# Sinkhorn attention, Fourier mixing and MLP on one core: every batch kept on chip, V made mean-free, the Fourier transform folded and taken along the sequence first, the MLP of one batch interleaved with the next

## Chip, cores and metric

One core of one Trainium2 chip. The metric is the device time of one execution in microseconds (us), the median of several runs; profiles are single executions. Engines are named as in the profile: PE is the matrix engine, PEld its weight load, DVE VectorE, ACT ScalarE, POOL GpSimd, SP SyncE. Line numbers such as L286 are lines of the kernel that was profiled, so an experiment with added lines has other numbers.

## The reference, cut to what matters

```python
B, H, S, D = 4, 8, 768, 64; n_blocks = 8; block = 96           # q, k, v are float32, 0.1 * randn
P = sort_net                                                    # [B, H, 8, 8]
for _ in range(5):                                              # Sinkhorn: softmax rows, then columns
    P = exp(P - max(P, -1)); P = P / sum(P, -1); P = P / sum(P, -2)
k_sorted = einsum('bhij,bhjcd->bhicd', P, k_blocks)             # mix the 8 blocks of a head
v_sorted = einsum('bhij,bhjcd->bhicd', P, v_blocks)
attn = softmax(q_block @ k_sorted_block.T / 8)                  # 96 x 96, block by block
x = (attn @ v_sorted_block) -> [B, S, 512]
mixed = real(fft(fft(x, axis=1), axis=2))                       # 768 x 512, per batch
u = x + mixed
un = (u - mean(u)) / sqrt(var(u) + 1e-6)
out = u + relu(un @ w_ch1) @ w_ch2                              # 512 -> 2048 -> 512
```

## The kernel before

It works in stages, each over all four batches. The mix matrices are built from the Sinkhorn result by 48 small copies between on-chip tiles. Mixed K and V go to DRAM and come back in another layout. The Fourier transform runs along the features first (tables of 257 columns, the rest mirrored), then along the sequence with all 768 rows as contraction. `u` goes to DRAM and is fetched again by the MLP, which is the last stage.

```python
    for t in range(2):                                  # mix matrices, by DMA
        for i in range(NB):
            e.dma_start(pc[:, i:i + 1], pw[16 * t:16 * t + 16, i:i + 1, :])
        nc.vector.memset(lpf, 0.0)
        for g in range(16):
            e.dma_start(lpf[8 * g:8 * g + 8, 8 * g:8 * g + 8], pc[8 * g:8 * g + 8, :])
    # ... q loaded and transposed ...
            for t in range(2):                          # K: rows are (b h i), columns (c d)
                nc.gpsimd.dma_start(cin, kv[128 * t:128 * (t + 1), :])
                for n in range(NTIL):
                    nc.tensor.matmul(ps, lhsPk[t], cin[:, 512 * n:512 * (n + 1)])
                    evict(n, oo[:, 512 * n:512 * (n + 1)], ps)
                nc.sync.dma_start(ks_dram[128 * t:128 * (t + 1), :], oo)
    # ... V the same in float32, with the sums over c for the mean path; back to vs_dram ...
            for b in range(B + 1):                      # attention, one batch behind its scores
                    nc.sync.dma_start(kssb[...], ks_dram[...])
                    nc.scalar.dma_start(vspb[...], vs_dram[...])
                # ... transposes, scores, exp - 1, eTm1 @ V, 1/sum, the mean put back ...
    # ... Fourier for each batch: 48 matmuls of 257 columns, then per 128 rows:
                for sc in range(6):
                    nc.tensor.matmul(pU, cs16_sb[:, sc, 128 * ic:128 * ic + 128],
                                     T1[b][:, sc, :], start=False, stop=False)
                    nc.tensor.matmul(pU, ssn16_sb[:, sc, 128 * ic:128 * ic + 128],
                                     T2[b][:, sc, :], start=False, stop=(sc == 5))
                nc.sync.dma_start(u_dram[6 * b + ic], u)
                # ... normalize, transpose into unT ...
    with tc.tile_pool(name="mlp", bufs=1) as mlp:       # the MLP of all batches, last
        for st in range(6):
            for fc in range(16):
                # 4 matmuls of 512 columns, relu on ACT
            for sc in range(4):
                # 16 matmuls of 512 columns
                nc.sync.dma_start(ur, u_dram[gidx])
                nc.vector.tensor_tensor(ot, pc2, ur, op=ALU.add)
```

The softmax here doesn't subtract the row's maximum and nothing guards it: scores larger than these inputs give would overflow.

## Time and profile before

539.37 us (median of 3 runs, 538.71 to 539.91).

| stage | stretch, us | PE busy, us | granted PE clock | what it is limited by |
|---|---|---|---|---|
| prologue: mix matrices, K and V mix, q transposes | 0 to 112 | 42.2 | 0.95 (no record before 60.1 us) | transfers, on the chain |
| attention | 112 to 232 | 91.6 | 0.50 | small matmuls at half clock |
| Fourier and normalization | 247 to 365 | 113.0 | 1.00 | PE |
| MLP | 365 to 536 | 165.8 | 1.00 | PE |

From the page of the kernel before, busy time by engine and slices of 1/40 of the span; a digit is the busy share in tenths, `PEclk` the granted clock:

```profile
PE 426.2 (80%) x2524; PEld 225.4 (42%) x2524; DVE 221.1 (41%) x750; ACT 184.7 (34%) x502; POOL 56.7 (11%) x85
...
PE   0500698127695959998999999998999999999996
...
PEclk9999999755555555559999999999999999999999
DMA  9999258799707073117951112122231313140502
```

PE is empty in places in the first fifth, at half clock in the second, and full after that. The table by stretch, kernel before:

```profile
core 0: us, PE busy (x) PEld busy (x) DVE busy (x) ACT busy (x) POOL busy (x), PEclk, DMA share, GB/s
0.00:112.00 112.00, 42.24 (x170) 19.44 (x170) 49.40 (x171) 26.24 (x79) 25.00 (x35) 0.95 1.06 195
112.00:232.00 120.00, 91.58 (x790) 60.52 (x792) 66.68 (x267) 57.30 (x155) 26.06 (x42) 0.50 0.52 62
247.00:365.30 118.30, 112.95 (x736) 65.43 (x736) 81.69 (x260) 42.83 (x169) 1.31 (x2) 1.00 0.37 100
365.30:535.70 170.40, 165.84 (x770) 74.97 (x767) 16.95 (x26) 57.47 (x98) 0.00 (x0) 1.00 0.25 75
```

What holds the prologue is read from the chain that ended last (start, length, what), kernel before:

```profile
1.26 14.71 DMA qsb_196<-in_q_dram
...
29.06 11.05 DMA pc_132<-pw
...
46.74 5.19 DMA lhsPf_141<-pc_132
...
103.79 7.90 DMA vspb_793<-vs_dram
112.10 6.32 DMA kssb_792<-ks_dram
```

These are a load of q, then the small copies that build the mix matrices and the way back from DRAM. The copies and the way back are the pieces that the change removes.

### The profile page before, as it was taken

Reading aid. Unit: us, or ns where it says so; the run is one execution under the profiler, and the core shown is the slowest. Engines: PE = TensorE matmul, PEld = TensorE weight load, DVE = VectorE, ACT = ScalarE, POOL = GpSimd, SP = SyncE. Lnnn points to the kernel's source line nnn. Section 1 sums busy time; section 2 is a strip of 40 time slices with the busy share of each in tenths; the row PEclk is TensorE's granted clock in tenths of the full one; section 3 lists DMA queues with packets and bytes.
Section 4 is the critical chain, followed back from the end, with each engine's and each line's share of the span. In section 5 each row is a group of like instructions: output and inputs, shape, how many; then the busy total and the mean of one; then the engine's idle time right before and its main releaser. Section 6 shows DMA issues by size and latency. Waiting matters only on the chain.

```text
span 535.7 us, 7003 instructions
## 1 busy us (share of the span) xinstructions
PE 426.2 (80%) x2524; PEld 225.4 (42%) x2524; DVE 221.1 (41%) x750; ACT 184.7 (34%) x502; POOL 56.7 (11%) x85
## 2 busy tenths in 40 slices
PE   0500698127695959998999999998999999999996
PEld 0300253014463645654646464643444444444442
DVE  1610589414474655865667676672111101010101
ACT  1400452019643719005514142325243333324240
POOL 5613000100041230541000000000000000000000
PEclk9999999755555555559999999999999999999999
DMA  9999258799707073117951112122231313140502
GB/s 319 196 198 112 89 185 319 169 118 147 48 2 59 1 56 115 49 50 221 202 138 51 69 61 77 42 80 98 46 113 40 118 39 119 21 137 6 152 0 80
DMA packets 95043, 55.46 MB, mean 104 GB/s; under 512 B 80664, under 2 KB 82720, under 8 KB 93472
## 3 DMA queue, kind: packets, MB, share of 16 engines
q1 hardware_dynamic: 35776, 29.53, 20.2%
q0 software_dynamic: 28416, 10.52, 16.6%
q10 hardware_dynamic: 30816, 14.96, 14.0%
q8 instruction: 20, 0.33, 0.3%
q14 instruction: 15, 0.12, 0.1%
HBM read 46.55 MB, written 18.94 MB: 122 GB/s over the span
## 4 chain that ended last, share of the span: by engine, by line
PE 67%; DMA 13%; DVE 9%; ACT 5%; issue 2%; ACTq 2%; SPq 1%; POOL 0%; DVEq 0%; POOLq 0%
DMA qsb_196<-in_q_dram 3%; DMA pc_132<-pw 2%; ACTq L288 2%; DMA vspb_793<-vs_dram 1%; DMA qsb_279<-in_q_dram 1%; DMA kssb_792<-ks_dram 1%; SPq L188 1%; DMA pc_159<-pw 1%; PE ps_2747 L386 1%; DMA lhsPf_141<-pc_132 1%; DMA vspb_2007<-vs_dram 1%; DMA vspb_1043<-vs_dram 1%; PE ps_5472 L499 1%; PE ps_5406 L499 1%; PE ps_5265 L499 1%
## 5 line engine op out<-in xcount | busy, mean ns | idle before, releaser
L491 PEld LDWEIGHTS <-w1sb 128*128 128x128 f16 x384 | 37.5, 98 | 45.1
L230 PE MATMUL ps_372<-pkin_369,lhsPk 128*128 128x512 f16 x1 | 0.6, 606 | 29.9 <-DVE lhsPk L220 29.9
L454 PEld LDWEIGHTS <-ssn_sb 128*128 128x128 f16 x144 | 14.1, 98 | 17.0
L452 PEld LDWEIGHTS <-cs_sb 128*128 128x128 f16 x144 | 14.0, 97 | 17.1
L230 PEld LDWEIGHTS <-lhsPk 128*128 128x128 f16 x12 | 1.5, 132 | 33.8 <-DVE lhsPk L220 30.2
L156 PE MATMUL ps_207<-ident,qsb_196 128*128 128x128 f16 x1 | 0.3, 289 | 16.0 <-DMA qsb_196<-in_q_dram 16.0
L156 PEld LDWEIGHTS <-kssb_792 128*128 128x128 f16 x24 | 2.5, 138 | 22.9 <-issue 22.9
L146 ACT CAST pkout_371<-ps_372 128x512 f16<-128x512 f32 x1 | 0.6, 585 | 32.9 <-DMA lhsPf_168<-pc_159 32.9
L220 DVE CAST lhsPk<-lhsPf_141 128x128 f16<-128x128 f32 x1 | 0.2, 227 | 27.0 <-DMA lhsPf_168<-pc_159 27.0
L156 PEld LDWEIGHTS <-qsb_196 128*128 128x128 f16 x24 | 2.1, 131 | 19.0 <-DMA qsb_196<-in_q_dram 19.0
L156 PE MATMUL ps_815<-ident,kssb_792 128*128 128x128 f16 x1 | 0.3, 266 | 12.2 <-DMA vspb_793<-vs_dram 12.2
L499 PEld LDWEIGHTS <-hr_5124 128*128 128x128 f16 x64 | 6.3, 98 | 7.5
L499 PEld LDWEIGHTS <-hr_4384 128*128 128x128 f16 x64 | 6.3, 98 | 7.5
L499 PEld LDWEIGHTS <-hr_4754 128*128 128x128 f16 x64 | 6.3, 98 | 7.5
L499 PEld LDWEIGHTS <-hr_4569 128*128 128x128 f16 x64 | 6.3, 98 | 7.5
L499 PEld LDWEIGHTS <-hr_4939 128*128 128x128 f16 x64 | 6.3, 98 | 7.5
L499 PEld LDWEIGHTS <-hr_5309 128*128 128x128 f16 x64 | 6.3, 98 | 7.5
L270 POOL DMA_DIRECT2D a_781<-a_dram x4 | 2.2, 567 | 55.5 <-DMA a_dram<-a_615 48.0
L505 DVE TENSOR_TENSOR ot_4500<-ps_4481,ur_4498 128x512 f32<-128x512 f32 x1 | 0.7, 692 | 17.0 <-PE ps_4481 L499 17.0
L505 DVE TENSOR_TENSOR ot_4685<-ps_4666,ur_4683 128x512 f32<-128x512 f32 x1 | 0.7, 692 | 16.6 <-PE ps_4666 L499 16.6
L505 DVE TENSOR_TENSOR ot_5055<-ps_5036,ur_5053 128x512 f32<-128x512 f32 x1 | 0.7, 692 | 16.6 <-PE ps_5036 L499 16.6
L505 DVE TENSOR_TENSOR ot_5425<-ps_5406,ur_5423 128x512 f32<-128x512 f32 x1 | 0.7, 692 | 16.6 <-PE ps_5406 L499 16.6
(2847 smaller groups left out, 1344.6 us busy)
## 6 DMA issues: line engine op xcount, KB each, us to landing
w1sb<-in_moe_w_ch_dram POOLq DMA_DIRECT2D x1, 2048.0 KB, 16.1
w2sb<-in_moe_w_ch_dram POOLq DMA_DIRECT2D x1, 2048.0 KB, 27.0
pvin_616<-in_v_dram SPq DMA_DIRECT2D x1, 1536.0 KB
pvin_656<-in_v_dram SPq DMA_DIRECT2D x1, 1536.0 KB
pkin_369<-in_k_dram POOLq DMA_DIRECT2D x1, 1536.0 KB, 12.6
pkin_409<-in_k_dram POOLq DMA_DIRECT2D x1, 1536.0 KB, 19.0
ks_dram<-pkout_371 SPq DMA_DIRECT2D x1, 1536.0 KB
ks_dram<-pkout_411 SPq DMA_DIRECT2D x1, 1536.0 KB
```

What stands on the lines that cost most here:

```text
L146: nc.scalar.copy(dst, src)
L156: nc.tensor.matmul(ps[:nn, :kk], src_ap, idt[:kk, :kk], is_transpose=True)
L188: e.dma_start(lpf[8 * g:8 * g + 8, 8 * g:8 * g + 8], pc[8 * g:8 * g + 8, :])
L230: nc.tensor.matmul(ps, lhsPk[t], cin[:, 512 * n:512 * (n + 1)])
L270: nc.gpsimd.dma_start(a16[:, b, :], asrc)
L288: nc.scalar.dma_start(vspb[:, h, :, 0:D], vs_dram[64 * b + 8 * h:64 * b + 8 * h + 8, :].rearrange("i (c d) -> c i d", d=D))
L386: nc.tensor.matmul(prs[32:64, :], atc[:, c, :], cd32_sb[:, c, :], start=(c == 0), stop=(c == 3))
L452: nc.tensor.matmul(pU, cs16_sb[:, sc, 128 * ic:128 * ic + 128], T1[b][:, sc, :], start=False, stop=False)
L454: nc.tensor.matmul(pU, ssn16_sb[:, sc, 128 * ic:128 * ic + 128], T2[b][:, sc, :], start=False, stop=(sc == 5))
L491: nc.tensor.matmul(ph, w1sb[:, mc, 128 * fc:128 * fc + 128], unT[mc][:, colr], start=(mc == 0), stop=(mc == 3))
L499: nc.tensor.matmul(pc2, hr[:, fc, 128 * sc:128 * sc + 128], w2sb[:, fc, :], start=(fc == 0), stop=(fc == 15))
L505: nc.vector.tensor_tensor(ot, pc2, ur, op=ALU.add)
```

## The change: intent and diff

The intent is to take transfers off the chain, to give PE less work, and to fill PE's gaps.

- **Key mix that transposes.** K is loaded with 128 partitions of (j, c) and multiplied by a mix matrix in which each entry of P is spread over a diagonal block. One matmul mixes and transposes, and nothing goes to DRAM. The mix matrices are built on DVE and POOL from masks.
- **Mean-free V.** The mean over each block's 96 rows is computed on DVE and subtracted. The small rest goes through the mix and attention in float16. The mean goes by a separate path into the rows that PE adds at the end.
- **Sequence-first Fourier with folded sums.** x(s) ± x(s+384) and x(d) ± x(512-d) are formed first, so both transforms have half the columns or half the contraction.
- **Order.** The work of a batch stays on chip, and `mlp(b-1)` is issued with the attention and Fourier of batch b. V is loaded in two halves (batches 0 and 1, batches 2 and 3) of two tiles each; these tiles share buffers with the MLP's hidden tile `hr`.

The diff, cut to its core (most of the kernel is rewritten; what is not shown has the same character):

```diff
-    for t in range(2):
-        ... 48 dma_start calls building lhsP from pw ...
+    for n, dst in ((0, tk), (1, tv)):
+        pdup = wt([32, NB, 128], F32, "r", 2, "pdup")
+        ... pw copied with repeats along 128 columns ...
+        for i in range(NB):
+            nc.tensor.matmul(ps[:, i, :], pdup[:, i, :], id32)
+        nc.vector.tensor_copy(dst, ps)
-                nc.sync.dma_start(ks_dram[128 * t:128 * (t + 1), :], oo)
-                    nc.scalar.dma_start(vs_dram[...], vo16)
+    def load_v(t, eng):
+        for hf in range(2):
+            tl = wt([128, 48, D], F32, "hr", 2, "v32")        # buffers of the MLP's hidden tile
+            eng[hf].dma_start(...)
+    def v_center(t):
+        for hf in range(2):
+            nc.vector.tensor_reduce(vs2[:, hf, :], vh[hf].rearrange("p c d -> p d c"), axis=AX.X, op=ALU.add)
+        ... vb = sum / 96 ...
+        vo = vc16[:, 0:D * BLK].rearrange("p (d r c) -> p c r d", r=6, c=16)
+        for hf in range(2):
+            eng = nc.vector if hf == 0 else nc.gpsimd
+            eng.tensor_tensor(
+                vo[:, 8 * hf:8 * hf + 8],
+                vh[hf].rearrange("p (c r) d -> p c r d", r=6),
+                vb[:, 0:1, :][:, None, :, :].broadcast_to([128, 8, 6, D]),
+                op=ALU.subtract)
+    def v_mix(t):
+                nc.tensor.matmul(ps[:, dd, :], vc16[:, BLK * d:BLK * d + 128],
+                                 bdv16[t].rearrange("p g i -> p (g i)"))
+    def attn(b):
+                    nc.vector.tensor_scalar(ed, ex..., -1.0, None, op0=ALU.add)   # into ebuf, exp - 1
+                        nc.tensor.matmul(po[:, 65 * T:65 * T + 65], e[...128 columns], vs[...])
+    def fft_ln(b):
+        nc.vector.tensor_tensor(p_[:, :, 0:DM], rt[:, 0:3, :], rt[:, 3:6, :], op=ALU.add)
+        nc.gpsimd.tensor_tensor(m_[:, :, 0:DM], rt[:, 0:3, :], rt[:, 3:6, :], op=ALU.subtract)
+        for n, src in ((0, p_), (1, m_)):
+            eng = nc.vector if n == 0 else nc.gpsimd
+            eng.tensor_tensor(t[:, :, 0:257], src[:, :, 0:257], src[:, :, DM:255:-1], op=ALU.add)
+            eng.tensor_tensor(t, src[:, :, 0:256], src[:, :, DM:256:-1], op=ALU.subtract)
+        ... 30 matmuls of 193 columns, then 5 of 512 for each 128 rows, u, normalization ...
+    v_center(0); v_mix(0); a_path(0); a_rows(0); attn(0); fft_ln(0)
+    load_v(1, ...); make_bdk(1); a_rows(1); attn(1); fft_ln(1)
+    v_center(1); v_mix(1); a_path(1)
+    mlp(0)
+    ... attn(2); fft_ln(2); mlp(1); attn(3); fft_ln(3); mlp(2); mlp(3)
```

The order of the calls is not the order in time: each engine has a list of its own.

The output `vo` has the index d, which runs fastest in the instruction, as its outermost axis. Neighbouring writes are therefore 96 elements, 192 bytes, apart. V mix then reads 128 neighbouring columns for one d.

## The prediction

> **What bounds the kernel now.** The slices and a table by stretch of the profile (535.7 us) show stages in sequence. 0-112 us is the prologue: PE is busy 42 us; the chain of waits is DMA (first q load 14.7 us, then 11 + 6 + 5.2 + 1.9 us of small copies building the mix matrices, then K and V back from DRAM, 7.9 + 6.3 us). 112-235 us is attention, 30 us a batch, at a granted PE clock of 0.50. 250-365 us is Fourier, PE 96% busy; 365-531 us is the MLP, PE 100% busy at 216 ns per 512-column matmul.
>
> **PE after.** MLP: same columns, 166 us. Fourier: a batch had 48 matmuls of 257 columns and 90 of 512 (some 25 us); it becomes 30 of 193, 30 of 512 and 24 transposes: 30*83 + 30*216 + 24*56 ns = 10.3 us, 41 us for four (pitch from the MLP; 56 ns per warm transpose from the timeline near 358 us). Attention: 232 small matmuls a batch, about 56 ns warm (13 us) or 107 ns at half clock (25 us). V mix 7 us, float32 rows 10 us. Sum, warm: about 276 us against 426.
>
> **Other engines** (estimates from durations in the trace: PSUM reads on DVE 0.16 us + 1.04 ns per element; exponential minus one 0.356 us; POOL two-input 0.61 us per 256 elements). DVE per batch: attention 17, Fourier and norm 22, MLP 4, rows 2 us; V twice 19 us; setup 12 us: about 230 us. ACT about 130, POOL about 75 us. DRAM round trips vanish.
>
> **Critical path.** A latency-bound head remains: V's first half (3.1 MB) shares the start with q, k, weights and tables, landing near 25 us; centring V (two 3072-element reductions, a subtraction split between DVE and slow POOL) to 42 us; V mix to 49; attention 0 at half clock, two heads in flight, to 74; Fourier and norm of batch 0, with POOL differences and a dozen tiny rsqrt operations per half batch, to 98. By then PE has done 40 of 276 us. Then the MLP of batch b-1 fills PE's waits in attention and Fourier b: 236 us if dense, plus 5 us tail: about 343 us. [...] I add 25 us because PE runs in its emitted order: a head's output matmul waiting for exponentials or a buffer holds the MLP matmuls behind it.
>
> **Prediction:** 368 us, range 335 to 415. Chances: faster 0.97, same 0.015, slower 0.015. Prologue and attention save about 100 us, Fourier about 70.
>
> **Right if:** PE busy near 280-300 us; first MLP matmul at 90-110 us; after it PE over 85% busy at clock 1.0; Fourier about 10 us of PE per batch; no large transfer on the chain after 30 us. **Wrong if:** the first MLP matmul starts after 120 us (V's buffers are shared with the MLP's hidden tile, so the second V half must be centred first; u has eight buffers, six held per batch); DVE and POOL slow each other [...] and DVE becomes the limit; strided writes cost more than the contiguous ones I costed; or attention stays at half clock beside the MLP. Then 400 us or more.

The sum: 98 us for the head, 236 of PE work and 5 of tail (given as "about 343"), and 25 for PE's waits, 368 us in all.

## The result, and the profile after

After: **455.61 us** (median of 4 runs, 454.41 to 455.85). Before, on the same chip in the same rounds: 539.59. The ratio is 0.845, with a 95% interval of 0.8429 to 0.847. Ratios in this text are the mean time of one kernel's runs over that of the other's of the same rounds, so they are not quite the ratios of the medians. Executions over 1.5% slower than the fastest of the same kernel are left out of the means.

So the kernel is faster, by 84 us instead of the 171 predicted, and the time lies outside the range of 335 to 415.

From the page of the kernel after, in the same form as before:

```profile
PE 309.8 (68%) x2420; PEld 182.3 (40%) x2420; DVE 302.2 (67%) x553; ACT 119.5 (26%) x264; POOL 136.1 (30%) x96
...
PE   0000065400366459996999999979999979999996
...
POOL 8390010499521910325500042290001082000000
PEclk9999999955555579999899999969999979999999
```

The PE work fell from 426 to 310 us, much as intended. The first five and later two more slices have no PE work at all. The table by stretch, kernel after (columns as before):

```profile
0.00:71.60 71.60, 7.04 (x33) 7.01 (x34) 56.82 (x46) 2.56 (x6) 27.31 (x24) 1.00 0.81 204
71.60:89.50 17.90, 11.71 (x124) 9.48 (x123) 16.55 (x30) 8.36 (x21) 5.00 (x10) 0.98 0.12 15
89.50:119.80 30.30, 0.00 (x0) 0.00 (x0) 30.30 (x4) 0.00 (x0) 30.12 (x1) 0.50 0.03 4
119.80:147.60 27.80, 18.34 (x206) 13.78 (x206) 18.37 (x47) 7.48 (x17) 4.76 (x6) 0.50 0.34 44
147.60:170.00 22.40, 11.05 (x61) 6.46 (x62) 15.98 (x32) 1.47 (x3) 12.61 (x8) 0.65 0.00 0
...
182.40:452.60 270.20, 249.85 (x1905) 138.53 (x1902) 154.59 (x370) 94.67 (x207) 55.46 (x48) 0.96 0.16 36
```

(The 1.00 in the first row is no measurement. The trace has no clock record before 75.1 us, and the view counts such time as full clock. The first V mix matmuls follow each other every 107 ns from 71.6 to 75.1 us and every 56 ns after it, so PE began at half speed.)

From 182 us on PE is busy 250 of 270 us: there the change does what it should. The loss lies ahead of the first MLP matmul, which starts at 172.9 us. In that head, three stretches are empty of useful PE work: 0 to 71.6, 89.5 to 119.8 (PE does nothing for 30 us), and half of 147.6 to 170. The chain of the kernel after names what ran then:

```profile
2.82 10.40 DMA v_85<-in_v_dram
13.24 5.28 DVE vs_0_212 L274
19.28 30.00 DVE vc_127 L286
49.30 13.08 DMA v_962<-in_v_dram
...
79.82 5.40 DVE vs_1_1576 L274
...
89.48 15.40 DVE vc_127 L286
104.88 14.97 DVE ebuf_119 L423
```

L286 is the subtraction of V's mean, L274 the sum over V, L423 the operation that writes exp - 1 in attention. The timeline of the kernel after (start, length, engine, what; in brackets the idle time before) shows how the two subtractions of one V half stand to each other:

```profile
19.14 15.45 POOL L286 TENSOR_TENSOR vc_127<-v_85,vb_215 128x3072 f16<-128x3072 f32 x1 [8.94 <-DVE vb_215 L280]
19.19 30.08 DVE L286 TENSOR_TENSOR vc_127<-v_83,vb_215 128x3072 f16<-128x3072 f32 x1
...
89.47 30.14 POOL L286 TENSOR_TENSOR vc_127<-v_964,vb_1579 128x3072 f16<-128x3072 f32 x1 [0.19 <-POOL rb_105 L347]
89.48 15.40 DVE L286 TENSOR_TENSOR vc_127<-v_962,vb_1579 128x3072 f16<-128x3072 f32 x1
...
104.45 15.39 DVE L423 TENSOR_SCALAR ebuf_119<-ex_403 96x384 f16<-96x384 f32 x1
119.77 0.47 DVE L423 TENSOR_SCALAR ebuf_119<-ex_411 96x384 f16<-96x384 f32 x1
```

Two things are to be read here. The one that starts first takes 15.4 us, and the other ends 15 us later although both were started together. And an operation that takes 0.47 us by itself takes 15.39 us when it starts while POOL is in its subtraction. Both look like one engine standing still for the whole length of the other's instruction. Yet even the first one, undisturbed, takes 15.4 us for 3072 elements per partition, 5.0 ns an element; at the prediction's rate for DVE (0.16 us and 1.04 ns an element) it would be 3.4 us.

The waits of PE, kernel after (in total, times, longest, us):

```profile
PE pf_180 L242 <- DVE pdup_178 L233: 57.1, 1, 57.1
PE pf_414 L431 <- DVE ebuf_119 L423: 31.3, 1, 31.3
```

`pdup` is the first step from the Sinkhorn result to the mix matrices. It comes at 56.4 us, because DVE's list has V's sums and subtraction in the middle of the five Sinkhorn iterations: four of the iterations stand behind the subtraction. Then the list has the first sum of V's *second* half, which waits until 62.4 us for its load, and only behind it the mix matrices. The chain puts the load's start down to the buffer that the first subtraction frees at 49.3 us; e2 will show that this buffer is not the only thing that holds it.

**The theories to be tested.**
- *Stride*: the subtraction is slow on either engine because it writes 2-byte elements 192 bytes apart.
- *Contention*: it is slow because DVE and POOL hold each other up; each alone would be fast.
- *Order*: the second V half, and V's work ahead of Sinkhorn, stand in DVE's list in front of what PE waits for.
- *Folds*: a smaller loss later on, from POOL's three sums ahead of each batch's Fourier stage (3.85, 1.8 and 1.9 us).

### The profile page after: what moved, and what is told of

Its sections match the earlier page's. It is cut to its first block, busy times and chain, and to the rows that moved or that the text cites. A ratio compares the mean times of both kernels' runs of the same rounds, so it can differ in the third digit from the quotient of the medians.

```text
span 452.6 us, 6022 instructions
## 1 busy us (share of the span) xinstructions
PE 309.8 (68%) x2420; PEld 182.3 (40%) x2420; DVE 302.2 (67%) x553; ACT 119.5 (26%) x264; POOL 136.1 (30%) x96
## 3 DMA queue, kind: packets, MB, share of 16 engines
q0 software_dynamic: 11040, 10.49, 15.4%
## 4 chain that ended last, share of the span: by engine, by line
PE 42%; DVE 40%; DMA 7%; POOL 4%; issue 4%; ACT 2%; SPq 0%; DVEq 0%; ACTq 0%
DVE vc_127 L286 10%; DVE ebuf_119 L423 5%; DMA v_962<-in_v_dram 3%; POOL pmt_135 L456 3%; DMA v_85<-in_v_dram 2%; DVE ebuf_121 L423 2%; DVE vsb_131 L307 1%; DVE vs_1_1576 L274 1%; DVE vs_0_212 L274 1%; PE pm_2760 L563 1%; PE pm_4167 L563 1%; PE pm_3821 L563 1%; PE pm_2895 L563 1%; PE pm_1969 L563 1%; PE pm_4013 L563 1%
## 5 line engine op out<-in xcount | busy, mean ns | idle before, releaser
L556 PEld LDWEIGHTS <-w1sb 128*128 128x128 f16 x512 | 48.8, 98 | 31.6 <-issue 1.0
L242 PE MATMUL pf_180<-id_sb,pdup_178 32*128 32x32 f32 x16 | 3.6, 397 | 57.1 <-DVE pdup_178 L233 57.1
L286 POOL TENSOR_TENSOR vc_127<-v_964,vb_1579 128x3072 f16<-128x3072 f32 x1 | 30.1, 30142 | 0.2 <-POOL rb_105 L347 0.2
L286 DVE TENSOR_TENSOR vc_127<-v_83,vb_215 128x3072 f16<-128x3072 f32 x1 | 30.1, 30080 | 0.0
L242 PEld LDWEIGHTS pf_180<-id_sb,pdup_178 32*128 32x128 f32 x16 | 3.5, 325 | 57.1 <-DVE pdup_178 L233 57.1
L431 PEld LDWEIGHTS <-ebuf_119 96*128 96x128 f16 x192 | 8.5, 105 | 43.1 <-DVE ebuf_119 L423 42.5
L286 POOL TENSOR_TENSOR vc_127<-v_85,vb_215 128x3072 f16<-128x3072 f32 x1 | 15.5, 15452 | 8.9 <-DVE vb_215 L280 8.9
L286 DVE TENSOR_TENSOR vc_127<-v_962,vb_1579 128x3072 f16<-128x3072 f32 x1 | 15.4, 15405 | 0.0
L423 DVE TENSOR_SCALAR ebuf_119<-ex_403 96x384 f16<-96x384 f32 x1 | 15.4, 15390 | 0.0
L218 ACT ACTIVATE pw<-pw 32x64 f32<-32x64 f32 x5 | 1.3, 255 | 51.2 <-DVE pw L225 50.1
L298 PEld LDWEIGHTS <-vc_127 128*128 128x128 f16 x128 | 9.9, 110 | 9.0 <-issue 8.1
L431 PEld LDWEIGHTS <-ebuf_121 96*128 96x128 f16 x192 | 8.7, 105 | 10.8 <-DVE ebuf_121 L423 10.3
L411 PEld LDWEIGHTS <-ksb_123 64*128 64x128 f16 x128 | 6.8, 100 | 7.6 <-issue 5.9
L567 DVE TENSOR_TENSOR u_3503<-pm_4129,u_3503 128x512 f32<-128x512 f32 x1 | 0.7, 691 | 13.2 <-PE pm_4129 L563 13.2
L411 PEld LDWEIGHTS <-ksb_125 64*128 64x128 f16 x128 | 7.0, 103 | 4.7 <-issue 3.2
L274 DVE TENSOR_REDUCE vs_1_1576<-v_962 128x64 f32<-128x3072 f32 x1 | 5.3, 5289 | 5.3 <-DMA v_962<-in_v_dram 5.3
## 6 DMA issues: line engine op xcount, KB each, us to landing
v_964<-in_v_dram SPq DMA_DIRECT2D x1, 1536.0 KB, 16.3
```

Source lines behind the costliest of these rows:

```text
L242: nc.tensor.matmul(ps[:, i, :], pdup[:, i, :], id32)
L274: nc.vector.tensor_reduce(vs2[:, hf, :], vh[hf].rearrange("p c d -> p d c"), axis=AX.X, op=ALU.add)
L286: eng.tensor_tensor(vo[:, 8 * hf:8 * hf + 8], vh[hf].rearrange("p (c r) d -> p c r d", r=6), vb[:, 0:1, :][:, None, :, :].broadcast_to([12 ...
L298: nc.tensor.matmul(ps[:, dd, :], vc16[:, BLK * d:BLK * d + 128], bdv16[t].rearrange("p g i -> p (g i)"))
L411: nc.tensor.matmul(ps[:, j, :], ks[rows, 4 * g + j].rearrange("p r c -> p (r c)"), qt[rows, :, cc])
L423: nc.vector.tensor_scalar(ed, ex.rearrange("p j r c -> p j c r"), -1.0, None, op0=ALU.add)
```

## The experiments

All kernels below gave correct results. The marks "V mix / first head / MLP" are the start of the first V mix matmul, the first output matmul of attention and the first MLP matmul, in us. In the kernel after they are 71.6 / 119.9 / 172.9. The kernel before had medians of 538.4 to 540.1 us in the four sets of runs.

### e1: both subtractions on DVE

```diff
-            eng = nc.vector if hf == 0 else nc.gpsimd
+            eng = nc.vector
```

> Edit: both halves of each V subtraction on DVE, none on POOL; the writes keep their 192-byte step. Theory S (stride): each half costs DVE about 15 us by itself because of the strided 2-byte writes, and the two engines already ran one after the other, so splitting bought nothing: four subtractions of 14.5 to 15.5 us, total within 2% of the changed kernel (446 to 464 us). Rival C (contention): alone a half costs about 3.4 us (1.04 ns an element) [...]: total 395 to 415 us.

Measured: 463.57 us (462.72 to 465.06), ratio 0.8602 (0.8564 to 0.8639); marks 85.5 / 127.6 / 182.8. The subtractions on DVE, without POOL's, take 15.39 to 15.48 us each, as long as POOL's took:

```profile
L286 DVE TENSOR_TENSOR vc<-v,vb 128x3072 f16<-128x3072 f32 x4 | 61.7, 15424 | 0.1
```

A copy on POOL that meets one of them, the kind that takes 0.82 us elsewhere in the same profile, takes 14.56 us (timeline of e1):

```profile
20.14 14.56 POOL L393 COPY qr<-q 128x768 f16<-128x768 f16 x1 [9.94 <-DMA q<-in_q_dram]
```

So the 15.4 us are not made by the two engines meeting: a rival that explains the slow subtraction by contention alone falls. The meeting costs something else. In the pairs measured here, the one that comes second takes about as long as both would in turn: 30.1 us where the first takes 15.4 (kernel after), 9.8 where each takes 6.65 and 3.35 when it is first (e2), 12.1 where it is 7.02 and 5.29 (e9). So it waits out the first one's whole instruction. Operations with one input did so too: the 14.56 us above, and 15.39 us for 0.47 in the kernel after. Not every operation does: e8 has a DVE reduction beside a POOL sum that took its usual time. What makes them wait, no trace shows.

That e1 as a whole is 8 us slower than the kernel after is not the subtraction: the first pair ends at 50.1 us, against 49.3. DVE's list came out in another order. `pdup` now stands behind both sums of the second half and comes at 75.5 us instead of 56.4.

### e2: the same values written in runs of 64

```diff
-        vo = vc16[:, 0:D * BLK].rearrange("p (d r c) -> p c r d", r=6, c=16)
+        vo = vc16[:, 0:D * BLK].rearrange("p (r c d) -> p c r d", r=6, c=16)
-                nc.tensor.matmul(ps[:, dd, :], vc16[:, BLK * d:BLK * d + 128], ...)
+                wv = vc16[:, 0:D * BLK].rearrange("p (m d) -> p d m", d=D)
+                nc.tensor.matmul(ps[0:96, dd, :], wv[:, d, :], ...)
```

> Edit: centred V is written as [position][channel], runs of 64 neighbours, split DVE/POOL as in the changed kernel; the matmul reads its weights with a step of 64 elements and 96 columns. Theory S: a half costs DVE 3.4 to 4 us and POOL 6 to 7 us; total 395 to 412 us, first MLP matmul at 120 to 130 us instead of 173. Rival C: the durations stay at 15 and 30 us, total 450 us or more.

Measured: 447.79 us (443.08 to 448.47), ratio 0.8287 (0.8234 to 0.834); marks 71.4 / 99.2 / 159.2. The subtraction falls from 15.4 to 3.35 us on DVE and to 6.65 us on POOL, where each was first to start. This is the plainest proof of the cause: same arithmetic, same reads, other addresses of the writes. The first pair now takes 9.8 us instead of 30.1. But the total missed its expectation of 395 to 412 by far, and the first V mix came no earlier. The timeline of e2 shows where the 20 us went:

```profile
62.18 5.28 DVE L274 TENSOR_REDUCE vs<-v 128x64 f32<-128x3072 f32 x1 [25.39 <-DMA v<-in_v_dram]
```

DVE stands still for 25 us in front of a sum over V's second half whose load has not landed; the mix matrices are further down its list. The buffer was free at 29 us, and still the load lands at 62, as in the kernel after. The chain of e2 says why:

```profile
13.14 9.34 SPq L175
...
22.83 20.92 SPq L175
...
43.86 18.29 DMA v<-in_v_dram
```

L175 issues the load of one small table row. SP is held at these two issues for 30 us, and V's second load is behind them in SP's list. It then takes 18.3 us, where the first load of V, of the same 1536 KB, took 6.7; the MLP's weights are in flight beside it (the load of the second of them, issued at 5.1 us, takes 57.6 us to land). So in the kernel after, whatever stands in DVE's list behind the first sum of the second half comes after 62 us, and the first slow subtraction, done at 49 us, is hidden behind that.

### e3 and e4: Sinkhorn first, without and with the runs of 64

Nothing is removed; V's sums are made to depend on the finished Sinkhorn result, so that they cannot stand ahead of it.

```diff
+        if t == 0:
+            for hf in range(2):
+                nc.vector.tensor_copy(vs2[0:32, hf, :], pw.rearrange("p i j -> p (i j)"))
         for hf in range(2):
             nc.vector.tensor_reduce(vs2[:, hf, :], ...)
```

> Edit: the reductions of V's first half wait for the finished normalised sort matrix (two 32x64 copies make the dependency), so that the 57 us wait of PE for the mix matrices goes; V's subtraction stays as slow. Theory: the mix matrices are ready near 25 us instead of 71, V mix starts at 55 to 60 us instead of 72, total 437 to 445 us. Rival (V's subtraction alone is the cause, the order does not matter): within 1% of the changed kernel.

> Both edits, contiguous writes and sort matrix first. Theory: V mix starts at 33 to 38 us, first MLP matmul at 110 to 118 us, total 388 to 398 us: the two effects overlap partly, as the short subtractions no longer hold the sort matrix up for long. If the slow subtraction were not the main cause: above 430 us.

Measured: e3 450.45 us (448.36 to 453.79), ratio 0.8358 (0.8297 to 0.8419), marks 58.9 / 114.4 / 169.7. e4 439.5 us (435.23 to 440.42), ratio 0.8137 (0.8086 to 0.8187), marks 38.6 / 90.9 / 150.8. Both missed their totals (437 to 445, and 388 to 398), and the gain of e3 is near the 1% that its rival allowed, though the V mix came 13 us earlier in e3 and 33 us earlier in e4. In e3 the V mix now comes right behind the slow subtraction (58.8 us). In e4 the V mix then broke off for 24 us: its evictions on DVE stood behind a sum over V's second half that waited for its load until 61.4 us. The wait was moved, not removed. Left in the head was the place of the second V half in DVE's list.

### e5: and the second V half behind attention of batch 0

```diff
+        if t == 1:
+            for hf in range(2):
+                nc.vector.tensor_copy(vs2[0:32, hf, :], rts[0][0:32, 0, D*3:D*3+D])   # h3; 7 in place of 3: h7
```

The second half's sums now depend on head 3 (h3) or on the last head (h7) of batch 0's attention. Both kernels also have the edits of e2 and e3.

> Edit: contiguous writes, sort matrix first, and the reductions of V's second half wait for head 3 of attention 0, so that DVE's queue no longer stands behind V's second load (25 us idle in the run with contiguous writes alone, 21 us in the run with both). Theory Q (after the stride, the order of DVE's queue is what holds the start): V mix runs without a break from 39 to 49 us, attention 0 starts near 50, first MLP matmul at 105 to 115 us, total 385 to 400 us. Rival P (something else in the start limits, the load itself or PE's half clock): no gain over the run with both edits, above 430 us.

> As the run before but V's second half waits for the last head of attention 0. Theory Q: attention 0 is shorter, its 14 us of DVE work for V falls into Fourier 0 and delays the norm: within 2% of the run before. A much larger difference would say that the place of this work in DVE's order matters more than its size.

Measured: h3 419.99 us (419.88 to 420.85), ratio 0.7793 (0.7773 to 0.7813), marks 38.5 / 61.7 / 131.7. h7 416.96 us (415.1 to 417.72), ratio 0.7728 (0.7702 to 0.7755), marks 38.6 / 61.7 / 130.6. The first head comes at 61.7 instead of 119.9 us. The totals are above the expected 385 to 400, and the first MLP matmul comes 17 us after the latest time expected (115). Where the rest is, e8 and e10 ask.

### e6 and e7: the order alone, and the writes with half the order

e6 has the order of e5_all_h3 with the writes 192 bytes apart; e7 has the writes in runs and the second half deferred to head 3, without Sinkhorn first.

> The two order edits with the strided writes kept: the 2 by 2 design's other corner. Theory: the stride still costs 30 us twice on the chain (V mix at 59 us, attention 0 broken by a 30 us lock), first MLP matmul at 145 to 158 us, total 425 to 440 us, 35 us or more above the run with all three. Rival (order alone explains the start): below 405 us.

> Contiguous writes and the deferred second half, without the sort matrix first. Theory: the sort matrix is held until 36 us by V's reductions and subtraction, mix matrices ready near 45 us instead of 28, so 5 to 9 us later than the run with all three: 393 to 407 us.

Measured: e6 450.35 us (448.08 to 452.58), ratio 0.8339 (0.8305 to 0.8372), marks 58.8 / 78.0 / 168.7. e7 427.22 us (426.65 to 428.94), ratio 0.7929 (0.7904 to 0.7954), marks 45.2 / 68.4 / 138.6. e6 missed its expectation of 425 to 440; its first MLP matmul came at 168.7 us, where 145 to 158 were expected. e7's first MLP matmul came 7 us behind e5_all_h3's, where 5 to 9 were expected, but its total missed 393 to 407, as e5_all_h3's had missed its own.

With e6 there is a square of four, given as ratios to the kernel before, since they come from several sets of runs:

| | order as changed | Sinkhorn first, second half deferred to head 3 |
|---|---|---|
| writes 192 bytes apart | 0.845 (after) | 0.8339 (e6) |
| writes in runs of 64 | 0.8287 (e2) | 0.7793 (e5_all_h3) |

A step of 0.01 in the ratio is 5.4 us. Each cure alone is worth 6 to 9 us, both are worth 35. They hide each other. With the slow writes, deferring the second half only moves its 30 us to another place where PE needs DVE: in e6 PE waits 44.5 us in all for `ebuf`, up to 16.3 at a time, behind the second half's work. With the old order, the fast writes end at a list that waits for a load (25.4 us in e2). The lock of which e6's expectation speaks is the pair at 89.5 us in the kernel after, 15.4 us on DVE and 30.1 on POOL.

### e8: POOL's three Fourier sums on DVE

```diff
-        nc.gpsimd.tensor_tensor(m_[:, :, 0:DM], rt[:, 0:3, :], rt[:, 3:6, :],
+        nc.vector.tensor_tensor(m_[:, :, 0:DM], rt[:, 0:3, :], rt[:, 3:6, :],
-            eng = nc.vector if n == 0 else nc.gpsimd
+            eng = nc.vector
```

> Edit on the changed kernel: the three Fourier sums that POOL makes (difference of the halves, its even and odd fold) go to DVE; all else as it was. Theory F: POOL's 3.85 + 1.8 + 1.9 us stand on the chain before each Fourier stage[...]: alone the six sums take 4 to 6 us of DVE per batch instead of 7.5 us in a chain, PE's wait before Fourier falls from about 4 us to 2 us or less and its clock drops less: 8 to 20 us off, total 436 to 447 us. Rival: DVE is loaded already, the sums only move and the total stays within 1% of the changed kernel.

Measured: 434.48 us (433.69 to 434.79), ratio 0.8038 (0.8017 to 0.806); marks 71.5 / 105.9 / 170.8. The gain is 21 us, at the upper end of the expected 8 to 20 and a little over it. One difference of 1536 float16 elements took 3.85 us on POOL, and takes 0.95 us on DVE. DVE's own folds had taken 2.85 to 3.33 us while POOL was in its sums. By itself DVE takes 0.56 us (kernel after, then e8, one line each of the view by source line):

```profile
L456 POOL TENSOR_TENSOR pmt_135<-r_984 x1: 3847/3847/3847, 209.0 to 209.0; 128x1536 f16<-128x1536 f16 x1
...
L462 DVE TENSOR_TENSOR ee_1367<-pmt_133 x1: 3327/3327/3327, 209.9 to 209.9; 128x771 f16<-128x771 f16 x1
```

```profile
L456 DVE TENSOR_TENSOR pmt<-r x4: 949/950/954, 149.6 to 351.0; 128x1536 f16<-128x1536 f16 x4
...
L462 DVE TENSOR_TENSOR ee<-pmt x8: 556/558/560, 150.5 to 352.8; 128x771 f16<-128x771 f16 x8
```

So all six sums of a batch take about 4.1 us on one engine (2 × 0.95 + 4 × 0.55), where two engines had needed some 7.6 (3.85, 1.79 and 1.90 in a row on POOL). In the steady part, from 162 to 428 us, PE is then busy 257 of 266 us at a clock of 0.99. POOL's time is 2.0 times DVE's for the float32 subtraction in runs (6.65 us against 3.35, e2). For the float16 sums the times above don't give the ratio, as POOL was held up too: in the kernel after, its 3.85 us begin 0.05 us after a DVE sum of 0.96 us has begun. If it stood behind that one, about 2.9 us are its own (estimate), 3.1 times 0.95. In e5_all_h7 one of POOL's folds met only a DVE reduction, which took its usual 5.35 us (timeline):

```profile
96.44 1.58 POOL L475 TENSOR_TENSOR oo<-pmt 128x768 f16<-128x768 f16 x1
```

This 1.58 us is 2.9 times DVE's 0.55.

### e9: the loop turned, the layout kept

Instead of giving `vc16` another layout, the subtraction can run through the same layout in the order in which it lies. Then it reads V with a step and writes eight neighbours (16 bytes) at a time.

```diff
-        vo = vc16[:, 0:D * BLK].rearrange("p (d r c) -> p c r d", r=6, c=16)
+        vo = vc16[:, 0:D * BLK].rearrange("p (d r c) -> p d r c", r=6, c=16)
-                vo[:, 8 * hf:8 * hf + 8],
-                vh[hf].rearrange("p (c r) d -> p c r d", r=6),
-                vb[:, 0:1, :][:, None, :, :].broadcast_to([128, 8, 6, D]),
+                vo[:, :, :, 8 * hf:8 * hf + 8],
+                vh[hf].rearrange("p (c r) d -> p d r c", r=6),
+                vb[:, 0, :][:, :, None, None].broadcast_to([128, D, 6, 8]),
```

> Edit on the changed kernel: the same subtraction into the same layout, but with the loop turned so that neighbouring elements are written one after the other (eight at a time) and V is read with a step. Theory S2 (it is the step of the 2-byte writes that costs, a step in the reads costs as in the reductions, 1.7 ns an element): 5 to 6 us a half on DVE, 6.5 to 8 us on POOL, total 445 to 452 us, as the run with contiguous writes. Rival (any step costs, reads as writes): 12 us or more a half, total 452 us or more.

Measured: 438.24 us (437.69 to 438.84), ratio 0.8111 (0.8089 to 0.8132); marks 71.5 / 102.1 / 156.0, better than the expected 445 to 452. The subtraction takes 5.29 us on DVE and 7.02 on POOL where each was first. Per element on DVE: 1.09 ns with both sides in runs, 1.72 ns with the *reads* far apart (1536 bytes), 5.0 ns with the *writes* far apart (192 bytes). On POOL the same three cases took 6.65 us (e2), 7.02 and 15.45 (kernel after), so reads far apart cost it 6%, and with writes far apart it is as slow as DVE. V mix keeps its 128 neighbouring columns: one weight load takes 98 ns (median, in e10), where in e11, with 96 columns at a step of 64, it takes 257.

### e10 and e11: all together

e10 is e9 (turned loop), Sinkhorn first, the second half deferred to the last head, and e8. e11 has the runs of 64 of e2 in place of the turned loop.

> All: turned loop, sort matrix first, second V half after attention 0, Fourier sums on DVE; V mix keeps 128 weight columns. Theory: 4 us less in V mix and 8 to 20 us less in the Fourier stages than the run of 417 us: 393 to 406 us.

> As the run before, with contiguous writes and 96 weight columns instead of the turned loop: 395 to 410 us; within 1.5% of it. The pair says whether the cheaper subtraction or the quicker weight load is worth more.

Measured: e10 **392.77 us** (391.5 to 393.62), ratio 0.7267 (0.7242 to 0.7291), marks 40.7 / 59.9 / 129.6. e11 399.54 us (399.36 to 400.18), ratio 0.7393 (0.7371 to 0.7415), marks 38.5 / 62.8 / 130.0. e10 is the fastest of all kernels here, 63 us ahead of the kernel after. e11 met its range of 395 to 410, but the two differ by 1.7%, over the 1.5% expected. The table by stretch, e10:

```profile
90.00:125.00 35.00, 9.98 (x59) 6.40 (x60) 34.00 (x42) 1.47 (x3) 12.14 (x6) 0.65 0.00 0
...
125.00:389.00 264.00, 256.24 (x2001) 141.91 (x1999) 157.94 (x408) 99.79 (x217) 33.78 (x40) 0.99 0.16 36
```

From 125 us on PE is busy 97% of the time. Before it, from 90 to 125 us, PE does 10 us of work and DVE 34: the second V half's sums (2 × 5.3 us) and subtraction now stand in front of batch 0's normalization. They have to, as the MLP's hidden tile needs their buffers. Of the 34 us, 6.97 are one operation of the normalization on 128 x 3 elements (at 107.7 us), which stands still for the whole of POOL's part of the subtraction. The wait, in the waits of PE of e10:

```profile
PE pf L550 <- DVE un L545: 25.6, 8, 22.3
```

### e12: the second V half loaded and centred behind the MLP of batch 0

```diff
-    load_v(1, [nc.sync, nc.sync])          # was ahead of attn(1)
     ...
-    v_center(1)
-    v_mix(1)
-    a_path(1)
     mlp(0)
+    load_v(1, [nc.sync, nc.sync])
+    v_center(1)
+    v_mix(1)
+    a_path(1)
```

(To e10, without its deferral to the last head, which the new place replaces. Two tiles of V's own would have been the cleaner test, but such a kernel did not build: its pool asks for 126.6 kB per partition, and the builder had 103.5 left.)

> e10_all_loop, with V's second half loaded, reduced, subtracted and mixed after batch 0's MLP instead of before it (so the shared V and hidden buffers no longer force it in front). Theory: of the 32 us by which e10's first MLP matmul (129.6 us) is still later than I predicted (98), about 20 are the second half's two reductions and its subtraction, which hold VectorE (34 of 35 us busy from 90 to 125) in front of batch 0's normalization. Then the first MLP matmul comes at 104 to 114 us, PE is busy over 18 of the 35 us from 90 to 125, and the median is 370 to 382 us. Rival: the normalization's own chain of small VectorE operations needs that time; then the first MLP matmul stays at 122 us or later and the median at 388 or more. A third possibility: the first MLP matmul comes early, but the second half's work now makes PE wait later; then first MLP under 114 and a median still over 385.

Measured: 400.32 us (398.6 to 401.0), ratio 0.7418 (0.7378 to 0.7459); marks 40.9 / 58.3 / 109.0: the first MLP matmul comes 20.6 us earlier than e10's. The third possibility of the expectation came true. In the same stretch PE now has 28 us of work in place of 10; the table by stretch, e12:

```profile
90.00:125.00 35.00, 28.10 (x228) 16.83 (x227) 24.26 (x70) 10.90 (x23) 7.30 (x9) 0.86 0.09 12
...
160.00:200.00 40.00, 22.04 (x116) 10.80 (x115) 28.03 (x57) 2.46 (x6) 5.78 (x1) 0.82 0.17 60
200.00:240.00 40.00, 31.86 (x323) 21.64 (x323) 22.00 (x52) 20.48 (x47) 14.08 (x12) 0.84 0.18 21
```

But the load now waits for a buffer that the MLP of batch 0 holds until 182 us, and PE loses more than it won: 18 us of 40 idle from 160 to 200, where e10 is busy 39 of 40, and 8 us more from 200 to 240. The waits of PE, e12:

```profile
PE pm L560 <- ACT hr L563: 21.3, 1, 21.3
PE pf L302 <- POOL vc L290: 20.7, 1, 20.7
```

The first of these is PE idle from 185.7 to 206.9 us: the MLP of batch 1 can't have its hidden tile until V's second half, which holds the buffer, has landed (188.3), been summed and been subtracted (206.4). It is as long as what was gained at the start. The second wait is for the *first* half's subtraction, 20 to 41 us, as in e10. So the place of the second half is what held the first MLP matmul back in e10, and as long as it shares its buffers with the hidden tile it has to be paid for on one side or the other.

### All runs

| kernel | median, us | ratio to before | V mix / first head / MLP, us |
|---|---|---|---|
| after | 455.61 | 0.845 | 71.6 / 119.9 / 172.9 |
| e1 both subtractions on DVE | 463.57 | 0.8602 | 85.5 / 127.6 / 182.8 |
| e2 writes in runs | 447.79 | 0.8287 | 71.4 / 99.2 / 159.2 |
| e3 Sinkhorn first | 450.45 | 0.8358 | 58.9 / 114.4 / 169.7 |
| e4 e2 + e3 | 439.5 | 0.8137 | 38.6 / 90.9 / 150.8 |
| e5_all_h3 e4 + second half behind head 3 | 419.99 | 0.7793 | 38.5 / 61.7 / 131.7 |
| e5_all_h7 the same behind the last head | 416.96 | 0.7728 | 38.6 / 61.7 / 130.6 |
| e6 order of e5_all_h3 alone | 450.35 | 0.8339 | 58.8 / 78.0 / 168.7 |
| e7 e2 + second half behind head 3 | 427.22 | 0.7929 | 45.2 / 68.4 / 138.6 |
| e8 Fourier sums on DVE | 434.48 | 0.8038 | 71.5 / 105.9 / 170.8 |
| e9 turned loop | 438.24 | 0.8111 | 71.5 / 102.1 / 156.0 |
| e10 e9 + order (last head) + e8 | 392.77 | 0.7267 | 40.7 / 59.9 / 129.6 |
| e11 the same with e2 for e9 | 399.54 | 0.7393 | 38.5 / 62.8 / 130.0 |
| e12 e10, second half behind the MLP of batch 0 | 400.32 | 0.7418 | 40.9 / 58.3 / 109.0 |

## Why the prediction was right or wrong

**Right.** The direction, and the savings in PE work: 310 us busy against 426, though a little over the 280 to 300 that I gave as a sign. The float32 matmuls that spread the Sinkhorn result (7.0 us) had not been in the sum. The DRAM round trips are gone (26.0 MB moved by the queues against 55.5). The interleaving works: from the first full MLP stretch on PE is busy 94% of the time (249.85 of 265.8 us between 182.4 and 448.2) at a clock of 0.97, so attention beside the MLP does not stay at half clock. In the kernel after, low clocks stand around and behind gaps of PE: 0.50 from 89.5 to 147.6 us, with the 30 us without a matmul, and 0.50 from 298 to 303 us, behind waits of 2.27 and 0.77 us. Idle time is not all of it: attention of batch 0 keeps PE busy 18.3 of 27.8 us at 0.50 (119.8 to 147.6), and attention in the kernel before 91.6 of 120 us. How dense the work must be for full clock, no run measures.

**Wrong: the head.** The prediction has the chain: V landed 25, centred 42, mixed 49, attention done 74, Fourier and normalization done 98. Measured in the kernel after, against it:

| step | predicted, us | measured, us | what the runs showed |
|---|---|---|---|
| V landed | near 25 | 13.2 | earlier than thought |
| V centred | 42 | 49.3 | the subtraction takes 30.1 us: 15.4 by its writes (e1, e2, e9), doubled by the wait for POOL's (timeline, e1) |
| V mix starts | 42 | 71.6 | mix matrices behind the load of V's second half (62 us) and behind Sinkhorn, and that behind V, in DVE's list (e2, e3, e4) |
| attention 0 done | 74 | 147.6 | second half's sums and subtraction ahead of head 0 (e5, e6, e7); with these gone still 86.5 (e12) |
| first MLP matmul | 98 | 172.9 | Fourier and normalization took 25 us, as predicted (24) |

**The step that failed** is "centring V (two 3072-element reductions, a subtraction split between DVE and slow POOL) to 42 us", together with what stood on it. Three terms were wrong.

1. *The size of V's operations.* The access pattern in the diff shows a 2-byte write with a step of 192 bytes, but the estimate used durations of contiguous operations. The chip took 15.4 us in place of the 3.4 that the prediction's rate gives. The sums, which read V 256 bytes apart, took 5.3 us each in place of 3.4. I named this as a thing that could prove me wrong and did not put a number on it. For DVE's writes it is 5.0 ns an element at that step (e1) against 1.09 in runs (e2).
2. *Splitting it between two engines.* I took DVE and POOL to work side by side. They took turns, so for the pair the split was worth nothing: 30.1 us, where DVE alone needs 2 × 15.4 (e1). The prediction names this too among the things that could prove it wrong, and puts no number on it. With the writes mended the split costs more than it saves: 9.8 us for the pair (e2) against 2 × 3.35, and 12.1 us (e9) against 2 × 5.29.
3. *What else is in the list.* The chain of the prediction has the first V half's work, then attention. DVE's list had the second V half in front of attention 0 too, and Sinkhorn behind the first. I had mentioned the shared buffers as a risk ("the second V half must be centred first"), but only for the MLP's start. That clause came true: e12 puts 20.6 us on it.

Terms 1 and 3 can't be added. Removing either alone gains 6 to 9 us, both together 35 (the square of e6). For the first MLP matmul, the sum is: 172.9 in the kernel after, 129.6 with writes, order and folds mended (e10), 109.0 with the second half out of the way (e12), 98 predicted. The last 11 us are in attention of batch 0, by the trace of e12. V mix lasts from 40.9 to 47.1 us (predicted 42 to 49). Then float32 matmuls of the mean's path, which the predicted chain left out, come first on PE until 53.2. Attention takes 33 us, to 86.5, where I had 25; Fourier and normalization take 22.5 us (predicted 24). The attention of e12 in the table by stretch:

```profile
53.20:86.50 33.30, 20.04 (x234) 14.84 (x232) 22.03 (x51) 9.41 (x21) 9.28 (x13) 0.59 0.38 51
```

PE is busy 20 of these 33 us at a low clock. How much of the 8 us is clock and how much waiting, no run separates.

**Wrong, and smaller: the steady part.** Predicted were 261 us from the first MLP matmul to the last (236 of PE work and 25 of waits), measured 275 (172.9 to 448.2). In the Fourier stages of batches 1 to 3 PE waited 3.1 to 4.1 us each for sums of POOL, and of DVE held up beside them, and part of a stage ran at half clock (0.50 from 298 to 303 us), although "POOL differences" were in the prediction. e8 removes that and gains 21 us; in e10 it is 258 us from the first MLP matmul at 129.6 us to the end of the last at 387.3. That agreement is partly luck: in these 258 us of e10 PE is busy 252, where I had 236, and waits 6, where I had allowed 25. Some of the extra work is in the four Fourier stages, which hold PE for 51 us in e8 where I had 41. The spacing of the matmuls was as I had it (83, 215 and 56 ns, medians in e8); what the other 10 us are was not measured. (The groups of e8's profile add up to 64 us for these stages, but they overlap: that sum counts the same time more than once.)

The total error is 88 us: 75 in the head, 14 in the steady part and about 2 behind the last matmul, less 4 by which the prediction's "about 343" exceeds its own parts (98 + 236 + 5 = 339).

**What stays open.** Whether the full 368 us can be reached: it would need buffers for V's second half that the MLP doesn't use, for which there is no room in this form. Why e2's V mix of 96 columns with a step is slow (257 ns a weight load against 98): the step and the number of columns were changed together. And what both subtractions on DVE would give once the writes are mended: e1 tried it only with the slow writes, and e2 to e12 all keep the split.

## What to carry to other kernels

For each element-wise instruction of a change, read the inner step of both access patterns in bytes before using a duration from a trace; a write with a step of 192 bytes cost DVE 4.6 times as much here (5.0 against 1.09 ns an element), and turning the loop so that the writes lie together and only the reads are apart got most of it back without a new layout (1.72 ns). Dividing the subtraction between DVE and POOL was no gain here, as one waited for the other (30.1 us for the pair, where DVE alone needs 2 × 15.4), and a short DVE operation behind it paid too (15.39 us for 0.47). And when a change shortens one link of a latency-bound head, follow each engine's list of instructions past it: two causes that hid each other gave 6 and 9 us here when mended one at a time, and 35 together.
